# A new timetable for rounding the weights, its last product on another engine, and fewer feed-forward pieces a turn

## Chip, cores and metric

The kernel runs on one core of a Trainium2 chip. The metric is the device time of one execution in microseconds (us). Every quoted time of an instruction comes from one profiled execution of the kernel before the change, or is worked out from it. The engines are called PE (matrix products), DVE (vector), ACT (scalar activations), POOL (GpSimd) and SP (the queue that issues most transfers).

## What is computed

```python
# attention: q, k, v of shape (4, 8, 768, 64), centroids (8, 16, 64)
q_assign = argmax(q_n @ c_n, -1);  k_assign = argmax(k_n @ c_n, -1)
mask   = q_assign[:, :, :, None] == k_assign[:, :, None, :]
scores = where(mask, q @ k.T / sqrt(64), -1e9)
attn   = softmax(scores)
x      = (attn @ v) brought to (3072, 512)      # 4 batches of 768 rows
# feed-forward layer: w_in (512, 2048), w_out (2048, 512)
h   = x @ w_in
out = h * sigmoid(1.702 * h) @ w_out
```

The inputs `q`, `k`, `v` and the centroids are 32-bit. The two weight matrices come as 64-bit floating-point numbers: the kernel reads each as two 32-bit halves and has to turn them into 32-bit numbers itself before a matrix product can use them. The code calls this rounding.

## The kernel before

**Attention runs in turns.** There are 16 pairs of heads (four batches of four pairs), and each pair has two halves of its 768 query columns, which gives 32 groups. A group has six key tiles. One turn handles two key tiles, so a group takes three turns and the loop over `t` runs 98 times, of which 96 start new tiles. The first 24 turns (`TB`) belong to batch 0. In a turn the kernel issues, in this order: the score products (L393), for batch 0 an additional product that carries the cluster mask (L407), the exponentials on ACT (L418), the mask on DVE for the later batches (L429) and the sum over key tiles on POOL (L439), pieces of the preparation of later pairs (transposes L271 with their ACT copies L276, `prep_near` L285 to L291, `prep_assign` L302 to L325), and the value products of the turn before (L450). Every third turn `normalise` closes a group: PE adds over partitions (L462), DVE takes the reciprocal (L465) and multiplies (L467). `check` then reads that reciprocal on ACT (L477, L479). In batch 0 it is called in the same turn as `normalise`, later one turn after it.

**The feed-forward work is filled in between.** When group 3 has been normalised (turn 13), 28 pieces of work for the first half of batch 0 go into the queue `half_ffn`: 16 calls of `first` (product L516, tanh on ACT L486, the factor on DVE L487) and 12 of `second3` (product L496). After group 7 (turn 25) 48 pieces for the second half go into `ffn`. A running account, `owed`, decides how many pieces a turn takes: it grows by `rate` a turn while `half_ffn` lasts and by 0.62 a turn for `ffn`, of which the last eight pieces are left until attention has ended. Batches 1 to 3 are computed after attention, by functions that the change does not touch.

**Rounding a weight piece.** The weights are cut into 32 pieces of 128 x 512, 16 of `w_in` and then 16 of `w_out`. One call of `round_next` is a round. Round i issues the load of piece i+2 on SP (L155), splits piece i, and joins piece i-1. The split is two DVE operations (L168 takes the exponent bits, L170 the leading mantissa bits) and two ACT operations (L172, L174). The join is three DVE operations: L180 adds the sign, L183 adds the low half, L186 multiplies the two parts. There are 33 rounds. The buffers are three for `raw` (a loaded piece) and two for `e` (its exponent). `first` and `second3` call `round_to`, which makes up rounds that are still missing for the columns or rows that they read.

**When rounds are issued.** Before turn 12 there is one round in turns 1, 2, 4, 5, 6, 8, 9 and 10, at the end of the turn. From turn 12 on there are two a turn (one right after the exponentials, one before the feed-forward pieces) and a third one in odd turns, after them. The 33 rounds end in turn 21. The engines take their instructions strictly in this written order, each engine by itself, and wait for each other by semaphores:

```python
        for u in us:
            exps(u)
        second_half = t >= TB // 2
        if second_half:
            round_next()
        if recs:
            check(*recs)
```

Of the kernel before, what the change touches and what calls it, by code (L numbers as in the profile page):

```python
# [8 lines left out]
FP32 = mybir.dt.float32  # L9
# [5 lines left out]
ALU = mybir.AluOpType  # L15
# [3 lines left out]
def kernel(  # L19
    tc: tile.TileContext,  # L20
    q: bass.AP,
    k: bass.AP,
    v: bass.AP,
    centroids: bass.AP,
    moe_w_in: bass.AP,
    moe_w_out: bass.AP,
    out: bass.AP,
):

    args = (q, k, v, centroids, moe_w_in, moe_w_out, out)
    bad = fast(tc, *args)
    with tc.If(bad > 0):
        general(tc, *args)
# [3 lines left out]
def fast(  # L39
# [26 lines left out]
    nc = tc.nc  # L66
# [7 lines left out]
    NH = NJ // 2  # L74
# [3 lines left out]
    NF = DF // P  # L78
# [73 lines left out]
    def load_w(i):  # L152
        if i < NW:
            t = wp.tile([P, WN, 2], I32, name="raw")
            nc.sync.dma_start(out=t.rearrange("p n t -> p (n t)"),  # L155
                              in_=w_chunks[i][1])
            w_raw[i] = t
# [5 lines left out]
    def split_w(i):  # L163

        hi = w_raw[i][:, :, 1]
        w = w_chunks[i][0]
        e = wp.tile([P, WN], I32, name="e", bufs=2)
        nc.vector.tensor_scalar(out=e, in0=hi, scalar1=EXP, scalar2=None,  # L168
                                op0=ALU.bitwise_and)
        nc.vector.tensor_scalar(out=w.bitcast(I32), in0=hi, scalar1=0xFFFFF,  # L170
                                scalar2=None, op0=ALU.bitwise_and)
        nc.scalar.activation(out=e, in_=e, func=AF.Relu, scale=8.0,  # L172
                             bias=low[:, 0:1])
        nc.scalar.activation(out=w, in_=w.bitcast(I32), func=AF.Copy,  # L174
                             scale=2.0 ** -20, bias=1.0)
        w_pow[i] = e

    def join_w(i):
        raw, e, w = w_raw.pop(i), w_pow.pop(i), w_chunks[i][0]
        nc.vector.scalar_tensor_tensor(  # L180
            out=e, in0=raw[:, :, 1], scalar=-2 ** 31, in1=e,
            op0=ALU.bitwise_and, op1=ALU.bitwise_or)
        nc.vector.scalar_tensor_tensor(  # L183
            out=w, in0=raw.bitcast(U32)[:, :, 0], scalar=2.0 ** -52, in1=w,
            op0=ALU.mult, op1=ALU.add)
        nc.vector.tensor_tensor(out=w, in0=w, in1=e.bitcast(FP32),  # L186
                                op=ALU.mult)

    w_done = [0]

    def round_next():
        i = w_done[0]
        if i < NW:
            load_w(i + 2)
            split_w(i)
        if 0 < i <= NW:
            join_w(i - 1)
        w_done[0] += 1

    def round_to(n):  # L200
        while w_done[0] <= min(n, NW):
            round_next()
# [50 lines left out]
    for a in range(2):  # L253
        rows = slice(a * D, (a + 1) * D)
        nc.vector.tensor_copy(
            out=cT[rows, :, a, :],
# [130 lines left out]
    def scores(u):  # L387
        g, kt = divmod(u, NJ)
        p, h = split(g)
        ps = ps_s.tile([P, 2, 512], FP32, name="s")  # L390
        for a in range(2):
            rows = slice(a * D, (a + 1) * D)
            nc.tensor.matmul(out=ps[:, a, 0:HALF],  # L393
                             lhsT=T[p, 1][rows, kt * P:(kt + 1) * P],
                             rhs=T[p, 0][rows, h * HALF:(h + 1) * HALF],
                             start=True, stop=(p >= HP))
        s_of[u] = ps[:, :, 0:HALF]

    def part(u):

        g, kt = divmod(u, NJ)
        p, h = split(g)
        if p >= HP:
            return
        for a in range(2):
            r = 32 * (2 * (p % 2) + a)
            nc.tensor.matmul(  # L407
                out=s_of[u][:, a, :],
                lhsT=hots[p // 2, 1][r:r + NC, kt * P:(kt + 1) * P],
                rhs=hots[p // 2, 0][r:r + NC, h * HALF:(h + 1) * HALF],  # L410
                start=False, stop=True)

    def exps(u):
        p, h = split(u // NJ)
        s = s_of[u]
        if p < HP:
            A_of[u] = ap.tile([P, 2, HALF], FP32, name="A")
        nc.scalar.activation(out=A_of[u] if p < HP else s, in_=s, func=AF.Exp,  # L418
                             scale=SCALE)

    def mask(u):

        g, kt = divmod(u, NJ)
        p, h = split(g)
        s = s_of.pop(u)
        if p >= HP:
            A_of[u] = ap.tile([P, 2, HALF], FP32, name="A")
            for a in range(2):
                nc.vector.scalar_tensor_tensor(  # L429
                    out=A_of[u][:, a, :],  # L430
                    in0=qcode[p][:, a, h * HALF:(h + 1) * HALF],
                    scalar=code[p][:, kt % NH, 1, kt // NH, a:a + 1],
                    in1=s[:, a, :], op0=ALU.is_equal, op1=ALU.mult)
        A = A_of[u]
        if kt == 0:
            return
        if kt == 1:
            sum_of[g] = ap.tile([P, 2, HALF], FP32, name="sum", bufs=2)
        nc.gpsimd.tensor_tensor(out=sum_of[g],  # L439
                                in0=A_of[u - 1] if kt == 1 else sum_of[g],  # L440
                                in1=A, op=ALU.add)

    def values(u):
        g, kt = divmod(u, NJ)
        p, h = split(g)
        if kt == 0:
            o_of[g] = ps_o.tile([P, 512], FP32, name="o")
        A = A_of.pop(u)
        for a in range(2):
            nc.tensor.matmul(out=o_of[g][a * D:(a + 1) * D, 0:HALF],  # L450
                             lhsT=v_in[p][:, a, kt, :], rhs=A[:, a, :],
                             start=(kt == 0), stop=(kt == NJ - 1))
        if kt == NJ - 1:
            O_of[g] = xp.tile([P, HALF], FP32, name="x")
            nc.scalar.copy(O_of[g], o_of.pop(g)[:, 0:HALF])
# [15 lines left out]
    recs = {}  # L471

    def check(g):


        rec = recs.pop(g)
        nc.scalar.activation(out=rec, in_=rec, func=AF.Copy,  # L477
                             accum_out=row_sums[:, 0, g:g + 1])
        nc.scalar.activation(out=rec, in_=rec, func=AF.Relu, bias=top[:, 0:1],  # L479
                             scale=-2.0 * LIMIT * LIMIT,  # L480
                             accum_out=row_sums[:, 1, g:g + 1])
# [22 lines left out]
    half_ffn, ffn = deque(), deque()  # L504
# [63 lines left out]
    NT = NU // 2  # L568
    TG = NJ // 2
    TB = 2 * HP * TG  # L570

    prep_at = {}
    for p in range(1, NPAIR):
        b, hp = divmod(p, HP)
        for i in range(2 if p == 1 else 0, len(PREP)):
            if p == 1:
                t = (i - 2) // 2
            elif b == 0:
                t = (hp - 2) * TG + 1 + i // 2
            else:  # L580
                t = b * TB + TG * hp - (7, 7, 6, 6, 4, 3, 2)[i]
# [5 lines left out]
    def prep(p, i):  # L587
        if i == 0 and p:
            load_v(p)
        PREP[i](p)  # L590
        if i in (1, 3) and loads:
            load_qk(*loads.popleft())

    rate = (NF + NH * (NF // 4)) / (TB / 2 - 0.5)
    owed = 0.0
    for p, i in [(0, i) for i in range(6)] + [(1, i) for i in range(2)]:
        prep(p, i)
# [2 lines left out]
    for t in range(NT + 2):  # L600
        us = range(2 * t, 2 * t + 2) if t < NT else ()
        for u in us:
            scores(u)
        if t == 0:
            prep(0, 6)
        for u in us:
            part(u)
        for u in us:
            exps(u)
        second_half = t >= TB // 2  # L610
        if second_half:
            round_next()
        if recs:
            check(*recs)
        for u in us:
            mask(u)
        work = sorted(prep_at.get(t, ()), key=lambda w: PREP[w[1]] != prep_near)
        while work and PREP[work[0][1]] == prep_near:
            prep(*work.pop(0))
        if 1 <= t <= NT:  # L620
            for u in range(2 * t - 2, 2 * t):
                values(u)

        todo = half_ffn or (ffn if len(ffn) > NF // 2 else ())
        owed += (rate if half_ffn else 0.62) if todo else -owed
        g = (t - 2) // TG if t >= 2 and (t - 2) % TG == TG - 1 else None
        if g is not None and second_half:
            normalise(g)
        for p, i in work:
            prep(p, i)  # L630
        if g is not None and not second_half:
            normalise(g)
        if recs and t < TB:
            check(*recs)
        if second_half or t and t % 4 != 3:
            round_next()
        while owed >= 1 and todo:
            todo.popleft()()
            owed -= 1
        if second_half and t % 2:  # L640
            round_next()
    check(*recs)
    qcode.clear()
    att.close()
# [181 lines left out]
    for b in range(1, B):  # L826
# [5 lines left out]
        for n in range(NH):  # L832
            sg = sums_g(n)
            if (b, n) == (B - 1, 1):
# [3 lines left out]
                                        op=ALU.min)  # L838
# [454 lines left out]
```

## Time and profile before

| what | value |
|---|---|
| median of three runs | 1054.43 us (1050.65 to 1055.23) |
| run that was profiled | 1050.77 us, span of its instructions 1048.9 us |
| PE busy | 996.9 us (95%) |
| DVE busy | 686.5 us (65%) |
| POOL busy | 389.3 us (37%) |
| ACT busy | 365.3 us (35%) |
| first turn starts / turn 14 / turn 27 / last turn | 11.4 / 87.7 / 253.5 / 582.8 us |

The first three rows are the clock of the whole kernel; the busy times are those of single engines in the profiled execution, and they overlap. The last row is read from the score products (L393) in the timeline, eight of whose records belong to a turn. A PE that is busy is not idle, but it can run at a reduced clock, so the granted clock has to be read beside it.

### The profile page before, as it was taken

The numbers are of one execution on the slowest core, as the hardware profiler recorded it, in microseconds if no ns is written. First come the engines' busy times: TensorE is split into PE (matmuls) and PEld (weight loads), VectorE is DVE, ScalarE is ACT, GpSimd is POOL, SyncE is SP. The second block draws the span as 40 slices with busy tenths as digits, with TensorE's granted clock in tenths as the row PEclk, the third lists the DMA queues.
The fourth block names the chain that finished last, engine by engine and source line by source line (L and its number), as shares of the span: only waits on it lengthen the run. The fifth ranks groups of instructions, "written<-read, shape, count | busy, mean of one in ns | idle before, by whom it ended". The sixth has DMA issues, their size and how long they took to land.

```text
span 1048.9 us, 12464 instructions
## 1 busy us (share of the span) xinstructions
PE 996.9 (95%) x4574; PEld 583.3 (56%) x4574; DVE 686.5 (65%) x1079; ACT 365.3 (35%) x697; POOL 389.3 (37%) x280
## 2 busy tenths in 40 slices
PE   7878798999999999999999899999999999999997
PEld 4323353445544455444554355688755788655886
DVE  3899998415876788776877667743477634576431
ACT  4655465324555455455555322200022200122000
POOL 2655222223666456655567847600022100120000
PEclk9998899999999999999999999999999999999999
DMA  8423354112002320022000000000000000000000
GB/s 219 130 64 117 120 158 139 35 53 63 17 0 63 82 71 8 25 70 59 26 1 1 1 11 0 1 21 21 21 0 1 1 21 21 21 0 1 21 21 23
DMA packets 66117, 45.24 MB, mean 43 GB/s; under 512 B 52096, under 2 KB 60032, under 8 KB 66048
## 3 DMA queue, kind: packets, MB, share of 16 engines
q1 hardware_dynamic: 65904, 44.33, 14.9%
q8 instruction: 38, 0.62, 0.3%
q14 instruction: 31, 0.25, 0.1%
q10 hardware_dynamic: 144, 0.03, 0.0%
HBM read 38.04 MB, written 6.31 MB: 42 GB/s over the span
## 4 chain that ended last, share of the span: by engine, by line
PE 82%; DVE 12%; ACT 3%; issue 1%; DMA 1%; POOL 1%; SPq 0%; DVEq 0%; ACTq 0%; POOLq 0%
PE b L790 21%; PE b L733 21%; PE s L393 11%; PE o L450 9%; PE m L496 8%; PE m L545 4%; DVE short L465 3%; PE m L516 2%; DVE A L429 2%; PE m L271 2%; PE m L462 2%; DVE e L168 1%; PE m L285 1%; DVE e L180 1%; DVE w_in L186 1%
## 5 line engine op out<-in xcount | busy, mean ns | idle before, releaser
L439 POOL TENSOR_TENSOR sum<-sum,A 128x768 f32<-128x768 f32 x128 | 235.8, 1842 | 199.8 <-DVE A L429 104.5
L429 DVE SCALAR_TENSOR_TENSOR A<-qb,code,s 128x384 f32<-128x384 uint8 x288 | 157.7, 608 | 94.7 <-ACT s L418 79.6
L393 PE MATMUL s<-T,T 64*128 64x384 f32 x768 | 157.1, 521 | 13.2 <-ACT A L418 9.0
L450 PE MATMUL o<-A,inv 128*64 128x384 f32 x768 | 147.1, 502 | 1.1 <-DVE A L429 1.1
L418 ACT ACTIVATE s<-s 128x768 f32<-128x768 f32 x144 | 109.4, 793 | 83.4 <-PE s L393 72.6
L724 DVE TENSOR_TENSOR G<-b,G 128x384 f32<-128x384 f32 x168 | 93.4, 556 | 51.8 <-PE b L733 45.0
L671 POOL TENSOR_TENSOR W<-w_in 128x256 f32<-128x256 f32 x24 | 17.7, 738 | 263.7 <-PE b L733 262.8
L393 PEld LDWEIGHTS s<-T,T 64*128 64x128 f32 x768 | 65.6, 188 | 86.2 <-issue 23.0
L724 DVE TENSOR_TENSOR y<-b,y 128x256 f32<-128x256 f32 x54 | 22.1, 423 | 130.0 <-PE b L790 93.8
L486 ACT ACTIVATE th<-G 128x384 f32<-128x384 f32 x96 | 50.2, 523 | 158.9 <-DVE G L724 98.4
L733 PE MATMUL b<-x,w_in 128*128 128x384 f32 x288 | 101.2, 486 | 0.0
L450 PEld LDWEIGHTS o<-A,inv 128*64 128x64 f32 x768 | 47.1, 137 | 86.7 <-issue 81.5
L439 POOL TENSOR_TENSOR sum<-A 128x768 f32<-128x768 f32 x32 | 59.6, 1863 | 92.6 <-ACT A L418 43.1
L465 DVE RECIPROCAL short<-m 128x384 f32<-128x384 f32 x32 | 81.7, 2553 | 13.7 <-PE m L462 13.6
L487 DVE SCALAR_TENSOR_TENSOR G<-th,G 128x384 f32<-128x384 f32 x96 | 68.6, 714 | 16.8 <-ACT th L486 14.2
L733 PEld LDWEIGHTS b<-x,w_in 128*128 128x128 f32 x288 | 54.7, 190 | 37.9 <-issue 0.5
L733 PE MATMUL b<-x,W 128*128 128x384 f32 x192 | 69.8, 486 | 0.0
L516 PE MATMUL m<-x,w_in 128*128 128x384 f32 x128 | 51.4, 560 | 15.5 <-ACT short L291 4.9
L790 PE MATMUL b<-Z,G 128*128 128x256 f32 x288 | 65.1, 379 | 0.0
L790 PE MATMUL b<-w_out,G 128*128 128x256 f32 x288 | 63.6, 379 | 0.0
L790 PEld LDWEIGHTS b<-w_out,G 128*128 128x128 f32 x288 | 54.6, 190 | 8.1
L496 PE MATMUL m<-w_out,g 128*128 128x512 f32 x120 | 58.7, 613 | 0.2 <-ACT T L276 0.2
(115 smaller groups left out, 1306.0 us busy)
## 6 DMA issues: line engine op xcount, KB each, us to landing
raw<-in_moe_w_in_dram SPq DMA_DIRECT2D x16, 512.0 KB, 3.6
raw<-in_moe_w_out_dram SPq DMA_DIRECT2D x16, 512.0 KB, 3.6
in<-in_q_dram SPq DMA_DIRECT2D x32, 192.0 KB, 3.0
in<-in_k_dram SPq DMA_DIRECT2D x32, 192.0 KB, 4.0
inv<-in_v_dram SPq DMA_DIRECT2D x16, 384.0 KB, 3.9
out_dram<-y SPq DMA_DIRECT2D x15, 256.0 KB, 2.1
qb<-line SPq DMA_DIRECT2D x12, 192.0 KB, 3.1
out_dram<-y SPq DMA_DIRECT2D x18, 128.0 KB, 1.8
```

Source lines behind the costliest of these rows:

```text
L393: nc.tensor.matmul(out=ps[:, a, 0:HALF], lhsT=T[p, 1][rows, kt * P:(kt + 1) * P], rhs=T[p, 0][rows, h * HALF:(h + 1) * HALF], start=True, ...
L418: nc.scalar.activation(out=A_of[u] if p < HP else s, in_=s, func=AF.Exp, scale=SCALE)
L429: nc.vector.scalar_tensor_tensor(out=A_of[u][:, a, :], in0=qcode[p][:, a, h * HALF:(h + 1) * HALF], scalar=code[p][:, kt % NH, 1, kt // NH ...
L439: nc.gpsimd.tensor_tensor(out=sum_of[g], in0=A_of[u - 1] if kt == 1 else sum_of[g], in1=A, op=ALU.add)
L450: nc.tensor.matmul(out=o_of[g][a * D:(a + 1) * D, 0:HALF], lhsT=v_in[p][:, a, kt, :], rhs=A[:, a, :], start=(kt == 0), stop=(kt == NJ - 1))
L465: nc.vector.reciprocal(out=rec, in_=ps[:, 0:HALF])
L487: nc.vector.scalar_tensor_tensor(out=g, in0=t, scalar=1.0, in1=h, op0=ALU.add, op1=ALU.mult)
L496: nc.tensor.matmul(out=ps[:, 0:DM], lhsT=g, rhs=w_out[:, f, :], start=(f == 0), stop=(f == NF - 1))
L516: nc.tensor.matmul(out=ps[:, 0:HALF], lhsT=w_in[:, c, f * P:(f + 1) * P], rhs=xT[c], start=(c == 0), stop=(c == NCH - 1))
L724: nc.vector.tensor_tensor(out=o, in0=p, in1=a, op=ALU.add)
L733: nc.tensor.matmul(out=ps[:, 0:HALF], lhsT=a[:, c], rhs=x(c), start=(c == 0), stop=(c == 1))
L790: nc.tensor.matmul(out=ps[:, 0:DN], lhsT=a(f // 4)[:, f % 4], rhs=z(f), start=(f == 0), stop=(f == FB - 1))
```

## The change

`join_w` is told which engine multiplies (L186): DVE up to turn 13, POOL from turn 14 on. The rounds follow a table, `pace`: one round in turns 0, 2, 5, 8, 9, 11, 12 and 13, then two rounds in every turn from turn 14 until all are done. A round of the first group stands right after the exponentials of its turn instead of at the end (turn 13: at the end); of the later pairs, one stands after the exponentials and one after the feed-forward pieces. The 33rd round falls in turn 26. The second call of `check` in batch 0's turns goes, so that `check` always runs one turn after `normalise`. `half_ffn` is taken at 1.6 pieces a turn instead of 28/11.5 = 2.43, which ends it in turn 31 instead of turn 25, and `ffn` at 0.65 instead of 0.62. The number of instructions of each kind is the same.

```diff
-    def join_w(i):
+    def join_w(i, engine):
         raw, e, w = w_raw.pop(i), w_pow.pop(i), w_chunks[i][0]
...
-        nc.vector.tensor_tensor(out=w, in0=w, in1=e.bitcast(FP32),
-                                op=ALU.mult)
+        engine.tensor_tensor(out=w, in0=w, in1=e.bitcast(FP32), op=ALU.mult)
...
-    def round_next():
+    def round_next(engine=nc.gpsimd):
...
-            join_w(i - 1)
+            join_w(i - 1, engine)
...
-    rate = (NF + NH * (NF // 4)) / (TB / 2 - 0.5)
+    rate = 1.6
+
+
+    pace = {t: 1 for t in (0, 2, 5, 8, 9, 11, 12, 13)}
+    pace.update((t, 2) for t in range(TB // 2 + 2, NT))
...
         second_half = t >= TB // 2
-        if second_half:
-            round_next()
+        dense = t >= TB // 2 + 2
+        if pace.get(t) and t != TB // 2 + 1:
+            round_next(nc.gpsimd if dense else nc.vector)
...
-        owed += (rate if half_ffn else 0.62) if todo else -owed
+        owed += (rate if half_ffn else 0.65) if todo else -owed
...
-        if recs and t < TB:
-            check(*recs)
-        if second_half or t and t % 4 != 3:
-            round_next()
         while owed >= 1 and todo:
             todo.popleft()()
             owed -= 1
-        if second_half and t % 2:
-            round_next()
+        if pace.get(t) == 2 or t == TB // 2 + 1:
+            round_next(nc.gpsimd if dense else nc.vector)
```

## The prediction, made before the changed kernel was run

> **What bounds the kernel now.** I read the slices of the span first, then busy times by stage cut at turn starts (turn 0 at 11.4 us, 14 at 87.7, 20 at 165.5, 27 at 253.5), then the waits, and last the timelines of PE, DVE and POOL where PE stands still. The slices:
>
> ```profile
> PE   7878798999999999999999899999999999999997
> DVE  3899998415876788776877667743477634576431
> POOL 2655222223666456655567847600022100120000
> PEclk9998899999999999999999999999999999999999
> ```
>
> A slice is 26 us. PE has room only in the first seven or so, up to about 190 us, and there DVE is full. The stages (columns: stretch, length, then PE, PEld, DVE, ACT, POOL, clock, DMA):
>
> ```profile
> 42.00:87.70 45.70, 36.65 (x205) 13.82 (x203) 42.44 (x50) 29.17 (x53) 26.51 (x13) 0.89 0.30 90
> 87.70:165.50 77.80, 67.17 (x252) 32.70 (x252) 74.40 (x103) 40.27 (x76) 23.22 (x12) 0.91 0.43 131
> 165.50:253.50 88.00, 81.84 (x329) 37.09 (x328) 39.05 (x60) 30.18 (x58) 21.22 (x12) 0.98 0.25 70
> 253.50:560.00 306.50, 300.15 (x1718) 146.91 (x1718) 236.06 (x362) 160.12 (x303) 185.62 (x104) 1.00 0.15 39
> ```
>
> From 42 to 253.5 us PE idles 9.1 + 10.6 + 6.2 = 25.8 us, and the clock withheld is worth 0.11 x 45.7 + 0.09 x 77.8 + 0.02 x 88 = 13.8 us more. After that PE sets the pace, so at most 39.6 us can be won, 3.8%. What PE waits for in this part, and what ACT waits for (turns 5 to 21):
>
> ```profile
> ACT e L172 <- DVE e L168: 24.1, 15, 3.1
> ACT short L477 <- DVE x L467: 21.9, 6, 4.4
> ...
> PE s L393 <- ACT A L418: 9.0, 4, 3.2
> ```
>
> DVE holds ACT, in rounding and in `check`, and ACT's exponentials then hold PE. Why DVE is full shows in its timeline beside POOL's (start, length):
>
> ```profile
> 63.20 3.85 POOL L439 TENSOR_TENSOR sum<-sum,A 128x768 f32<-128x768 f32 x2 [2.78 <-ACT A L418]
> 63.47 1.92 DVE L168 TENSOR_SCALAR e<-raw 128x512 int32<-128x512 int32 x1
> 65.31 2.03 DVE L170 TENSOR_SCALAR w_in<-raw 128x512 int32<-128x512 int32 x1
> 67.27 0.67 DVE L180 SCALAR_TENSOR_TENSOR e<-raw,e 128x512 int32<-128x512 int32 x1
> ```
>
> L168 and L170 take 0.42 us by their medians; here each lasts until one of POOL's two sums ends. DVE's rounding and POOL exclude each other.
>
> **What the Trainium skill says.** "SBUF — State Buffer", section Who interferes with whom: a GpSimd operation and a DVE one with two SBUF inputs, or in a two-port mode, take turns, each for its whole length; DVE operations with one SBUF input and no such mode are free. The trace agrees: 1.92 against 0.42 us, while the reciprocal (2.55 us) and the mask (0.609 us) keep their length beside POOL. "GPSIMD Engine Reference", section 3.1, gives some 2.5 cycles an element for two inputs; here 768 elements take 1.812 us and 256 take 0.727, 2.1 ns an element. "Perfetto Trace Analysis", section Optimizing Scalar/DVE Operations, warns that moving work between these two engines might not help. "TensorE: Matmul & The Clock Gate", Part 1, halves PE's clock after an idle window of about 3.4 us; here a turn's score products take 2.93 us after a 3.0 us gap at 63.1 us, against 1.56.
>
> **The change part by part.**
>
> *Prices.* A round on DVE takes 2.72 us from start to start (41.86 to 44.58 us): split 0.68, L180 and L183 1.31, L186 0.73. The product on POOL is in no trace: between the two widths above, 512 elements give 0.727 + 256 x 2.12 ns = 1.27 us; the rows of POOL that read `w_out` take 1.048 for 256, which would give 1.59. Nothing excludes a shorter time, but no row is faster per element. I take 1.27. A gelu factor (L487) is 0.56 us, a `normalise` 3.2, an assignment 2.2, a mask 0.61 on DVE; a sum 1.81 on POOL.
>
> *How far POOL and DVE overlap.* From 87.7 to 165.5 us: 17 rounds 46.2, 12 factors 6.7, three normalisations 9.6, 12 sums 21.7: 84.2 us in 77.8. So 6.4 of POOL's 21.7 us (30%) lay beside DVE work.
>
> *Turns 0 to 13.* Before, 13 rounds are issued, now 8: five less, 13.6 us of DVE. But turns 5, 8 and 11, each after a `normalise`, now have the round right behind the exponentials, so that ACT's L172 waits for DVE as `check` did. Turn 5: reciprocal from 38.1 us, its product to about 41.3, then L168 and L170 each behind a sum, to 45 or 46; ACT then does L174, `check` (1.5 us) and the copies to 48.5, which `prep_near` on PE needs; before, that product started at 48.39. Turns 8 and 11 by the same steps let turn 10 start at 66.7 (before 67.9), turn 13 at about 81.3 (83.5) and turn 14 at 85.7 (87.7). So moving `check` behind the exponentials gives almost nothing, and the stage gains 2 us; nothing is lost unless round 0 is too early for its data. Its load is issued at 7.8 us and L168 could start at 14.7 us; landing takes 3.6 us on a quiet queue. Bounds: 0 to 2 us; I take 0, since turn 1's late rounds had nothing to wait for either. On SP the load of piece 2 moves ahead of one load of a pair that is transposed only in turn 4. The larger gain is in what DVE owes: x of group 3 is ready at 89 us, against 96.8 before, and no `first` has to wait for it.
>
> *Turns 14 to 26, the block that decides.* DVE, from the end of `normalise`(3): 24 splits and 25 joins without product 16.3 + 32.8, round 7 still on DVE 2.7, 16 factors 9.0, four normalisations 12.8, two assignments 4.4, 12 masks 7.3: 85.3 us. POOL: 22 sums 39.8 and 25 products 31.8: 71.6. In series that is 157 us; with 30% of POOL beside other work, 135. The least is 157 minus the DVE work that POOL does not hinder (factors, reciprocals, masks, most of the assignments: 30 us), 127. PE in the same turns: ten times 3.57 and three times 3.07 for attention, 16 `first` at 2.67, four `second3` at 3.45, normalising 3.2, transposes and assignment of pairs 4 to 7 15.9: 120.4 us, less than DVE with POOL.
>
> *A wait is added.* With two buffers for `e`, L168 of round i needs POOL's product of piece i-2, which is issued in the round just before. The second round of a turn is followed on DVE by the first of the next, so L168 waits at least 1.3 us, and behind it every later DVE operation and ACT's L172. It is the time for which the shared port would have held L168 anyway, so I count it once. POOL's sums queue behind the products; they are wanted two turns later, so that costs nothing. Pieces of `w_in` are ready turns ahead of their `first`; the last `second3` of the first tile, in turn 26, reads piece 31 of the same turn: 0 to 2 us, 0.5 taken.
>
> *Sum.* 135 us from 89 end at 224 for DVE; PE's turn 27 needs no rounding any more and can start some 7 us earlier, at 216.5. Eight `second3` (27.6 us) and one piece of `ffn` (2.0) are still to be done there that were done before: 246.1 against 253.5, 7.4 us less. From turn 27 to 31 PE has 10 us of work a turn, DVE half, so nothing is lost; the pace 0.65 lets `ffn` reach turn 92 instead of 88 and may save 1 us of the bare turns at the end. In all about 8 us: 1041 against the span of 1048.9. The profiled run (1050.8) lies at the low end of the three; against their median, 1054.4 - 8.4 = 1046.
>
> **The rivals.** *PE keeps the pace.* If POOL's products fall beside reciprocals, masks and DVE's waits for PE, the block takes PE's 120.4 from 85.7: turn 27 at 206, 235.7 against 253.5, 18 less: 1036; with the stalls of turns 6 to 12 gone as well, 1027. For it: DVE is then often waiting, and POOL is free in that time. Against: PE has only 1.1 us to spare a turn.
>
> *DVE and POOL in series: slower.* L168 behind the product of the round before, and that product behind the sums in POOL's order, leave no overlap. Then the block takes 157, turn 27 starts at 238, and 267.7 against 253.5 is 14 more: 1068; with products of 1.59 us, 1076. It decides from where less than 20% of POOL's time is beside other work (143 us for the block). For it: the added wait ties every second product to DVE. Against: the 30% measured before.
>
> *It evens out.* 20 to 28% overlap, or half-clock stretches at small gaps in turns 14 to 19: 1050 to 1059. That the change fails to do what it says I exclude: it moves named instructions.
>
> **How the numbers follow.** The main case (1040 to 1052) gets 0.48, PE's pace 0.22, evening out 0.12, series 0.18. Of the main case 0.10 lies within 0.5% (5.3 us, about what a measurement of this kernel can tell from no change), 0.38 below. Faster: 0.38 + 0.22 = 0.60; the same: 0.10 + 0.11 = 0.21; slower: 0.01 + 0.18 = 0.19. The range reaches into both outer cases, to 1028 and 1064, and leaves out the lowest of the one and the upper half of the other, about 0.14. Main case alone: 1040 to 1052.
>
> **What would show it.** Right: turn 14 starts at 84 to 87, turn 27 at 212 to 221, turn 32 near 263; products on POOL of 1.2 to 1.6 us; L168 idle or stretched by about 1.3 us once a turn; `first` no longer waiting for L467. Wrong: turn 27 after 224 (series), or before 209 with PE without gaps (PE's pace); or a gain in turns 0 to 13 above 5 us, which would mean that `check` had mattered.

## The result and the profile after

The changed kernel takes 1065.74 us (median of four runs, 1065.08 to 1068.97), the one before 1054.79 us. The ratio is 1.0119, with a 95% interval of 1.0086 to 1.0152: it is slower by some 12.5 us. The execution that was profiled is the slowest of the four (1068.97 us, span 1067.2), and the profiled one of before lay near its fastest, so the two traces are 18.3 us apart. What follows accounts for these 18.3; what an edit wins or loses is taken from the ratios.

The slices of the changed kernel, in the order of those shown above:

```profile
PE   7788796889999999999999899999999999999997
DVE  3567855584467687777777757743477725476432
POOL 2444554443356556665566757700022100121000
PEclk9889987899999999999999999999999999999999
```

In the first nine slices, up to 240 us, DVE is nowhere full now (3 to 8), and PE in one of them alone. The stages, cut at this kernel's own turns (turn 14 starts at 97.0 us, 27 at 245.3, 32 at 292.5; columns as before):

```profile
42.00:97.00 55.00, 45.81 (x253) 17.63 (x249) 38.95 (x39) 29.01 (x52) 30.24 (x17) 0.88 0.23 63
...
97.00:245.30 148.30, 124.05 (x500) 57.25 (x498) 94.79 (x151) 71.21 (x135) 74.45 (x48) 0.90 0.38 114
...
245.30:292.50 47.20, 46.96 (x175) 19.76 (x174) 22.93 (x34) 12.58 (x23) 14.54 (x9) 1.00 0.08 25
```

The middle row is the block of turns 14 to 26. PE is idle for 24.3 of its 148.3 us, and a clock of 0.90 takes up to another 14.8 us (an estimate, 0.10 of 148.3); DVE works for 94.8 and POOL for 74.5 us. No single engine is the bound. Against before:

| start of | before | after | difference |
|---|---|---|---|
| turn 2 | 21.9 | 22.9 | +1.0 |
| turn 4 | 32.7 | 39.7 | +6.9 |
| turn 14 | 87.7 | 97.0 | +9.3 |
| turn 27 | 253.5 | 245.3 | -8.1 |
| turn 32 | 278.2 | 292.5 | +14.4 |
| last turn | 582.8 | 601.3 | +18.5 |

Of the first line 0.4 us lie before turn 0. Part of the fourth is spread between executions: turn 14 starts between 93.3 and 98.0 us in the other kernels below whose turns 0 to 13 are those of the changed kernel, and in `slow_pace`, which has those of before, at 89.9. The block is 17.5 us shorter than before, but it leaves eight `second3` and one piece of `ffn` to later turns, whose stage grows by 22.5 us (47.2 against 24.7). The tail, from turn 32 on, gives a little back.

Two stalls of PE show the two causes. The first is in turn 2. The timeline of PE, then that of DVE:

```profile
26.96 0.55 PE L270 MATMUL m<-ident,in 128*128 128x128 f32 x3
31.99 0.90 PE L270 MATMUL m<-ident,in 128*128 128x128 f32 x3 [4.48 <-DVE qb L362]
```

```profile
25.41 0.42 DVE L168 TENSOR_SCALAR e<-raw 128x512 int32<-128x512 int32 x1
25.76 0.42 DVE L170 TENSOR_SCALAR w_in<-raw 128x512 int32<-128x512 int32 x1
26.09 2.31 DVE L180 SCALAR_TENSOR_TENSOR e<-raw,e 128x512 int32<-128x512 int32 x1
28.33 2.29 DVE L183 SCALAR_TENSOR_TENSOR w_in<-raw,w_in 128x512 f32<-128x512 uint32 x1
30.65 0.69 DVE L186 TENSOR_TENSOR w_in<-w_in,e 128x512 f32<-128x512 f32 x1
31.37 0.56 DVE L362 COPY qb<-m 64x768 bf16<-64x768 bf16 x1
```

(Lines of the changed kernel are one lower from L186 on, up to the feed-forward part.) PE's transposes wait for a PSUM bank (PE writes its results into PSUM, and a bank must be copied out before it is written again) that the copy L362 of `prep_hot` must empty. Round 1 now stands in front of that copy, and two of its operations are held by POOL's sums (2.31 and 2.29 us instead of 0.68).

The second is in turn 20. ACT's timeline, then PE's line at its end:

```profile
161.87 0.72 ACT L172 ACTIVATE e<-e,low 128x512 int32<-128x512 int32 x1 [4.58 <-DVE e L168]
162.50 0.61 ACT L174 ACTIVATE w_out<-w_out 128x512 f32<-128x512 int32 x1
163.02 1.49 ACT L417 ACTIVATE A<-s 128x768 f32<-128x768 f32 x2
165.21 0.72 ACT L172 ACTIVATE e<-e,low 128x512 int32<-128x512 int32 x1 [0.70 <-DVE e L168]
165.84 0.61 ACT L174 ACTIVATE w_out<-w_out 128x512 f32<-128x512 int32 x1
...
167.61 0.46 ACT L290 COPY short<-m 128x384 f32<-128x384 f32 x1
```

```profile
168.12 1.65 PE L515 MATMUL m<-x,w_in 128*128 128x384 f32 x2 [6.41 <-ACT short L290]
```

ACT does its part of the second round of turn 19, the exponentials, its part of the first round of turn 20, then `check`, and only then the copies L290 and L275 that give PE its banks back. Each part of a round waits for DVE's split, and that one for POOL (DVE's waits in the block):

```profile
DVE x L486 <- ACT x L485: 30.2, 9, 7.5
DVE e L168 <- POOL w_out L186: 9.7, 7, 1.4
DVE e L168 <- POOL w_in L186: 5.5, 4, 1.4
```

PE, ACT, DVE and POOL hand the turn round in a ring, and each stands still for part of it. Of the 24.3 us that PE is idle in the block, 20.3 are waits of the feed-forward products (L515, L495) for L290 or L275.

### The profile page after: what moved, and what is told of

Its sections match the earlier page's. It is cut to its first block, busy times and chain, and to the rows that moved or that the text cites. A ratio compares the mean times of both kernels' runs of the same rounds, so it can differ in the third digit from the quotient of the medians.

```text
span 1067.2 us, 12458 instructions
## 1 busy us (share of the span) xinstructions
PE 1007.6 (94%) x4574; PEld 586.1 (55%) x4574; DVE 659.8 (62%) x1054; ACT 364.8 (34%) x697; POOL 418.6 (39%) x305
## 4 chain that ended last, share of the span: by engine, by line
PE 84%; DVE 9%; ACT 3%; issue 2%; POOL 2%; DMA 0%; DVEq 0%; ACTq 0%; POOLq 0%
PE b L790 20%; PE b L733 20%; PE s L392 11%; PE o L449 10%; PE m L495 8%; PE m L544 4%; PE m L515 3%; PE m L270 2%; DVE e L168 2%; PE m L461 2%; DVE short L464 2%; PE m L284 1%; DVE e L180 1%; POOL w_out L186 1%; PE m L295 1%
## 5 line engine op out<-in xcount | busy, mean ns | idle before, releaser
L671 POOL TENSOR_TENSOR W<-w_in 128x256 f32<-128x256 f32 x24 | 17.7, 739 | 263.7 <-PE b L733 263.2
L464 DVE RECIPROCAL short<-m 128x384 f32<-128x384 f32 x32 | 81.7, 2552 | 12.2 <-PE m L461 12.1
L486 DVE SCALAR_TENSOR_TENSOR G<-th,G 128x384 f32<-128x384 f32 x96 | 68.4, 713 | 17.1 <-ACT th L485 14.4
L515 PE MATMUL m<-x,w_in 128*128 128x384 f32 x128 | 54.2, 581 | 18.5 <-ACT short L290 10.1
L790 PE MATMUL b<-w_out,G 128*128 128x256 f32 x288 | 63.6, 379 | 0.0
L495 PE MATMUL m<-w_out,g 128*128 128x512 f32 x120 | 60.0, 625 | 3.3 <-ACT T L275 3.3
```

The source lines that it names most:

```text
L464: nc.vector.reciprocal(out=rec, in_=ps[:, 0:HALF])
L486: nc.vector.scalar_tensor_tensor(out=g, in0=t, scalar=1.0, in1=h, op0=ALU.add, op1=ALU.mult)
L495: nc.tensor.matmul(out=ps[:, 0:DM], lhsT=g, rhs=w_out[:, f, :], start=(f == 0), stop=(f == NF - 1))
L515: nc.tensor.matmul(out=ps[:, 0:HALF], lhsT=w_in[:, c, f * P:(f + 1) * P], rhs=xT[c], start=(c == 0), stop=(c == NCH - 1))
L790: nc.tensor.matmul(out=ps[:, 0:DN], lhsT=a(f // 4)[:, f % 4], rhs=z(f), start=(f == 0), stop=(f == FB - 1))
```

## The experiments

Each kernel's ratio is to the kernel before, run on the same chip in between, with its 95% interval. The changed kernel stands at 1.0119.

**The early rounds.** In `early_end` the rounds of turns 0 to 12 go back to the end of their turns; in `late2` only that of turn 2.

```diff
-        if pace.get(t) and t != TB // 2 + 1:
-            round_next(nc.gpsimd if dense else nc.vector)
+        if dense and pace.get(t):
+            round_next(nc.gpsimd)
...
-        if pace.get(t) == 2 or t == TB // 2 + 1:
+        if pace.get(t) and (not dense or pace[t] == 2):
             round_next(nc.gpsimd if dense else nc.vector)
```

> The changed kernel with the rounds of turns 0 to 12 at the end of their turns, where the kernel before had its early rounds; the calendar and all else stay. Theory 1 (the round of turn 2 stands in front of pair 1's hot copy on DVE, and PE waits 4.5 us for a bank): turn 3 starts at 27 to 28 us instead of 32.8, and 5 to 7 us are kept to the end: about 1059. Theory 2 (what counts is the dense part alone, and time lost early is taken back there because DVE catches up): turn 14 starts earlier, but the end moves by less than 2 us: 1064 to 1066.

1.0017 (1.0007 to 1.0027), 1054.8 us: theory 1, and some 4 us more than it asked for. Turn 3 starts at 26.8 us and turn 14 at 82.0 instead of 97.0, and the block then takes 147.8 us as in the changed kernel. The copy stands in front of the round again:

```profile
25.66 0.56 DVE L362 COPY qb<-m 64x768 bf16<-64x768 bf16 x1 [0.82 <-PE m L357]
26.25 0.59 DVE L168 TENSOR_SCALAR e<-raw 128x512 int32<-128x512 int32 x1
```

> The changed kernel with the round of turn 2 alone at the end of its turn; the rounds of turns 0, 5, 8, 9, 11 and 12 stay right behind the exponentials. Theory 1 (in the early stage turn 2 is the loss: its round delays a PSUM bank that PE waits for): turn 3 starts at 26 to 28 us, and 5 to 7 of the 11 us come back, 1059 to 1061. Theory 2 (rounds right behind the exponentials hold ACT in turns 5, 8 and 11, and turn 2 only shifts that): 1064 to 1066 although turn 3 starts earlier.

1.0058 (1.0039 to 1.0077), 1060.1 us: about half of it. Turn 14 starts at 90.0 us. That is theory 1: turn 2 costs about 6 us. The other half of what `early_end` won, about 5 us, lies in the rounds right behind the exponentials of the other early turns. Three stalls of PE in turns 6, 9 and 12, of 2.6, 3.5 and 2.9 us in the changed kernel, are the same in `late2` within 0.1 us and shrink to 1.4, 2.3 and 2.3 us in `early_end`; the second is, in the changed kernel:

```profile
74.35 2.35 PE L392 MATMUL s<-T,T 64*128 64x384 f32 x8 [3.53 <-ACT A L417]
```

**Who multiplies.** `dve_mult` puts all products on DVE, `mult2_dve` only that of a turn's second round.

```diff
 # dve_mult
-        engine.tensor_tensor(out=w, in0=w, in1=e.bitcast(FP32), op=ALU.mult)
+        nc.vector.tensor_tensor(out=w, in0=w, in1=e.bitcast(FP32), op=ALU.mult)
 # mult2_dve
         if pace.get(t) == 2 or t == TB // 2 + 1:
-            round_next(nc.gpsimd if dense else nc.vector)
+            round_next(nc.vector)
```

> The changed kernel with the last product of every piece on DVE again (0.7 us there instead of 1.27 us on POOL); calendar and pace stay. Theory 1 (PE, ACT and DVE run in turn, because ACT's copies stand behind both rounds' ACT part; the product on POOL lengthens the loop once a turn by about 1.4 - 0.7 us): 13 turns by 0.7 make 5 to 9 us less, 1057 to 1061. Theory 2 (POOL relieves a DVE that is full, so giving the product back costs 25 by 0.7 us): up to 10 us more, 1070 to 1076.

> The changed kernel with the product of every second round of a turn on DVE, so that the exponent of the next round no longer waits for a POOL product issued just before; the product of the first round stays on POOL. If the added wait is what costs: 13 turns by 0.7 us or more, 1053 to 1057. If the loop through ACT stays as long as it is without that wait, or the waiting is passed on to the shared port: 1063 to 1066.

`dve_mult`: 1.0198 (1.0176 to 1.022), 1073.5 us, so theory 1 as stated falls; the number is that of theory 2, but not, as `order_only` below shows, for its reason. `mult2_dve`: 1.0003 (0.9989 to 1.0018), 1053.5 us: the added wait does cost what was supposed. L168's waits for POOL, 15.2 us, are gone, and the block takes 136.8 us instead of 148.3. The product of the second round on POOL is a loss of some 12 us, that of the first round a gain of some 20. A saving of 13 times 0.7 us of DVE doesn't explain 20, so I formed another theory: the first round's product stands in POOL's order in front of the turn's sums. It waits for DVE's join, and so the sums start only when DVE has done with its round and no longer hold its operations. Without it, in `dve_mult`, a sum starts beside the round (a line of POOL, then two of DVE):

```profile
129.61 3.76 POOL L438 TENSOR_TENSOR sum<-sum,A 128x768 f32<-128x768 f32 x2 [8.19 <-ACT A L417]
...
129.80 1.92 DVE L168 TENSOR_SCALAR e<-raw 128x512 int32<-128x512 int32 x1
131.64 2.02 DVE L170 TENSOR_SCALAR w_in<-raw 128x512 int32<-128x512 int32 x1
```

`order_only` tests that. It is `mult2_dve` with 496 of 512 columns of the first round's product on DVE as well; POOL multiplies the last 16.

```diff
-        engine.tensor_tensor(out=w, in0=w, in1=e.bitcast(FP32), op=ALU.mult)
+        f, k = e.bitcast(FP32), WN if engine is nc.vector else WN - 16
+        nc.vector.tensor_tensor(out=w[:, 0:k], in0=w[:, 0:k], in1=f[:, 0:k],
+                                op=ALU.mult)
+        if k < WN:
+            engine.tensor_tensor(out=w[:, k:], in0=w[:, k:], in1=f[:, k:],
+                                 op=ALU.mult)
```

> The changed kernel with the second round's product on DVE, and of the first round's product 496 of 512 columns on DVE too; only the last 16 columns are left to POOL. Theory 1 (the first round's product on POOL helps because it stands in front of the sums in POOL's order, so that the sums start after DVE's join and do not hold its operations; where the work is done matters little): near the run with whole products there, 1053 to 1059, against 1073.5 with all products on DVE. Theory 2 (it helps because it takes 0.7 us of work a turn from DVE): near the run with all products on DVE, 1069 to 1074.

1.0009 (0.9994 to 1.0024), 1054.4 us: with hardly any of the multiplying left on POOL the gain is whole. The groups of DVE in the block, first of `dve_mult`, then of `order_only` (count, then busy us and mean ns):

```profile
L180 DVE SCALAR_TENSOR_TENSOR e<-raw,e 128x512 int32<-128x512 int32 x26 | 22.6, 870 | 0.0
L168 DVE TENSOR_SCALAR e<-raw 128x512 int32<-128x512 int32 x25 | 21.0, 841 | 0.4
L170 DVE TENSOR_SCALAR w_out<-raw 128x512 int32<-128x512 int32 x16 | 13.1, 820 | 0.0
L170 DVE TENSOR_SCALAR w_in<-raw 128x512 int32<-128x512 int32 x9 | 8.6, 958 | 0.0
```

```profile
L180 DVE SCALAR_TENSOR_TENSOR e<-raw,e 128x512 int32<-128x512 int32 x26 | 17.8, 683 | 0.0
L168 DVE TENSOR_SCALAR e<-raw 128x512 int32<-128x512 int32 x25 | 12.0, 481 | 0.4
L170 DVE TENSOR_SCALAR w_out<-raw 128x512 int32<-128x512 int32 x16 | 6.7, 418 | 0.0
L170 DVE TENSOR_SCALAR w_in<-raw 128x512 int32<-128x512 int32 x9 | 5.4, 598 | 0.0
```

The same instructions, 65.3 us against 41.9. The sums now meet other operations of DVE, such as L471 (1.24 us by its mean, against 0.59 for the same one, L466, in `dve_mult`), but those are few. The timeline of `order_only`, one line of DVE and then POOL's:

```profile
151.05 0.68 DVE L187 TENSOR_TENSOR w_out<-w_out,e 128x496 f32<-128x496 f32 x1
...
151.09 0.71 POOL L190 TENSOR_TENSOR w_out<-w_out,e 128x16 f32<-128x16 f32 x1 [6.85 <-DVE w_out L183]
151.76 3.69 POOL L443 TENSOR_TENSOR sum<-sum,A 128x768 f32<-128x768 f32 x2
```

The prediction quoted a warning that moving work between these two engines might not help. Here the same work helped in one place of the turn and harmed in the other.

**The place of the dense round.** A dense turn is one with two rounds, 14 or later. `prep_first` issues the first round of turns 14 and later behind the preparation steps, so that ACT's copies and `check` go first.

```diff
-        if pace.get(t) and t != TB // 2 + 1:
-            round_next(nc.gpsimd if dense else nc.vector)
+        if pace.get(t) and t < TB // 2 + 1:
+            round_next(nc.vector)
...
             prep(p, i)
+        if dense and pace.get(t):
+            round_next(nc.gpsimd)
```

> The changed kernel with the first round of a dense turn (14 on) issued behind the preparation steps and before the feed-forward pieces, so that ACT copies the transposes and runs check before its part of that round; the product stays on POOL. Theory 1 (PE waits for banks whose ACT copies stand behind the round): the waits of the feed-forward product for those copies, some 20 us in turns 17 to 25, go to under 6, the block of turns 14 to 26 falls from 148 to 130 to 138 us, 1050 to 1056. Theory 2 (the exponent's wait for POOL's product sets the block wherever the round stands): tanh and factor then stand behind the round instead, the block stays at 144 to 150, 1062 to 1067.

1.0056 (1.0038 to 1.0074), 1058.5 us, and a block of 138.3 us: nearer to theory 1, without reaching its time. PE's waits for L290 and L275 fall from 20.3 to 11.9 us in the feed-forward products, but 4.1 us appear before the transposes, and the sums reach DVE's rounding again: L168, L170, L180 and L183 together take 78.2 us in the block instead of 64.0.

**The pace of the pieces.** `fast_rate` takes the changed kernel back to 28/11.5 and 0.62; `slow_pace` gives the kernel before 1.6 and 0.65.

```diff
-    rate = 1.6
+    rate = (NF + NH * (NF // 4)) / (TB / 2 - 0.5)
...
-        owed += (rate if half_ffn else 0.65) if todo else -owed
+        owed += (rate if half_ffn else 0.62) if todo else -owed
```

> The changed kernel with 28/11.5 pieces a turn for the first half-block and 0.62 for the second, as before the change. Theory 1 (a turn with two rounds takes 10 to 11 us whatever PE has to do, so fewer pieces a turn leave PE idle): PE is filled in turns 14 to 25, its idle time between 98 and 245 us falls from about 25 us to under 10, and the end comes 8 to 16 us earlier, 1050 to 1058. Theory 2 (the port shared by POOL and DVE sets the block, and the gelu factors only add to it): the turns become longer by as much as PE gains, 1063 to 1068.

1.0194 (1.0174 to 1.0215), 1073.2 us: worse than either theory said, for a reason in neither. The pieces overtake the calendar of rounds (`pace`), `round_to` makes the missing rounds up in front of `second3`, and PE waits for each product on POOL:

```profile
PE m L495 <- POOL w_out L186: 14.9, 7, 5.6
```

PE is idle for 22.9 us between 98 and 245 us, not for under 10. So this run doesn't decide between the theories; it shows that the pace is tied to the calendar.

> The kernel before with the new pace of the feed-forward pieces alone (1.6 and 0.65), its own rounds and products. Theory 1 (fewer pieces a turn leave PE with nothing to do while a DVE-bound turn lasts): the turns of the rounds get hardly shorter, because rounds and not factors fill DVE; 6 to 12 us more, 1060 to 1066. Theory 2 (spreading the half-block into turns in which PE has room is a gain by itself): 1 to 5 us less than before, 1048 to 1053.

1.0073 (1.0056 to 1.0091), 1060.2 us: theory 1 by its number, though the turns did get shorter. With the rounds of before, the slower pace alone is a loss of 7 to 8 us: turn 27 comes 17.7 us earlier, but with some 29 us more of PE work still to do.

**`check`.** `check_late` takes only the second call of `check` from the kernel before.

```diff
-        if recs and t < TB:
-            check(*recs)
```

> The kernel before without its second call of check in batch 0's turns, so that check follows one turn after the normalisation; nothing else. The prediction's step (nothing to win, since the round behind the exponentials holds ACT in the same way) was argued with the new places of the rounds; with the old places, at the end of the turn, theory 1: the exponentials of the next turn no longer stand behind the reciprocal, the three stalls of 2.4 to 3.2 us before turns 6, 9 and 12 shrink, and 3 to 8 us are won, 1045 to 1050. Theory 2: DVE's backlog passes the wait to ACT's part of the rounds: within 2 us of before.

1.0023 (1.0014 to 1.0031), 1055.7 us: theory 2, with a small loss of some 2 us. The stalls move from before turns 6, 9 and 12 to before turns 6, 10 and 12 (1.5, 2.7 and 2.3 us), and another of 2.7 us stands before turn 14.

**Together.** `combo` has the edits of `early_end` and `mult2_dve`, `combo_prep` that of `prep_first` as well, and `before_order` brings the finding on POOL's order into the kernel before, in the first round of turns 12 and later, all else as it was.

```diff
 # before_order; in join_w the product is split as in order_only
         if second_half:
-            round_next()
+            round_next(WN - 16)
```

> The changed kernel with both edits of the runs before: rounds of turns 0 to 12 at the end of their turns, and the product of a turn's second round on DVE. If early and dense stage lose independently (11 and 12 us by those runs), their gains add: 1042 to 1046. If they share a cause, such as time lost early being waited out later, the gain is that of one alone: 1052 to 1055.

> The best kernel so far (early rounds at the end of the turn, second round's product on DVE, 1043) with the first round of a dense turn behind the preparation steps. If the waits of the feed-forward product for ACT's copies in turns 17 to 25 (12 us still) come from the round standing in front of those copies: 4 to 9 us less, 1034 to 1039. If the place of POOL's product in front of the sums mattered more, which this edit gives up: 1043 to 1050.

> The kernel before, with the last 16 of 512 columns of the product left to POOL in the first round of every turn from 12 on; rounds, pace and check as before. Theory 1 (a product in front of the sums in POOL's order keeps the sums off DVE's rounding, whatever else the change does): DVE's round operations between 88 and 254 us lose most of the 18 us by which sums lengthen them, and 6 to 14 us are won, 1040 to 1048. Theory 2 (this works only with rounds spread as in the changed kernel; here a third round in odd turns and DVE's backlog let the sums collide with another round): within 3 us of before.

`combo`: 0.9903 (0.9884 to 0.9922), 1043.0 us: the two losses are independent and their gains add. `combo_prep`: 0.9906 (0.9887 to 0.9925), 1042.6 us: nothing on top. Its block takes 136.4 us, `combo`'s 137.6 and `prep_first`'s 138.3, so two edits that each shorten the block don't add. They may shorten the same ring; but `combo_prep` also gives up the place in front of the sums, and L168, L170, L180 and L183 take 74.8 us in its block against 63.6 in `combo`. No run keeps the two apart. `before_order`: 0.9921 (0.9906 to 0.9936), 1045.0 us: sixteen columns on POOL are worth 8 us without anything else of the change. The sums' hold on DVE shrinks less than theory 1 asked for, though: the round operations between 87.7 and 253.5 us take 80.2 us, with two more of them in that stretch, instead of 84.8.

## Why the prediction was wrong

*What bounds the kernel* fits the runs: relieving DVE of POOL's sums alone won 8 us (`before_order`). *The price of the product on POOL* was right (1.27 us against medians of 1.270 for `w_in` and 1.272 for `w_out` in the trace).

*Turns 0 to 13* failed. The prediction had turn 14 at 85.7 us, 2 less than before; it came at 97.0. Its step "nothing is lost unless round 0 is too early for its data" looked at the wrong round and the wrong resource. Round 0 did little harm (turns 0 and 1 take 11.1 us instead of 10.5); round 1, moved in turn 2 ahead of `prep_hot`, kept PE waiting 4.5 us for a bank. That instruction stood in the same turn of the code, and I had not listed what queues behind the moved round on DVE there. For turns 5, 8 and 11 I had found that ACT's part of the round takes over `check`'s wait, and counted that as even with before. That much held for `check` (`check_late`), but not for the rounds: the ends of the turns were worth some 5 us more (`late2` against `early_end`). So x of group 3 was ready at 100.3 us, not at 89.

*The block* failed in its method. I added DVE's and POOL's work, let 30% overlap as measured before, and took the 135 us for the time, since PE had less. From 85.7 us that put turn 27 at 216.5, 130.8 us for the block; it took 148.3. The 30% came from a stage in which DVE was full. Here DVE waited 30.2 us for tanh and 15.2 for POOL's products, and the sum of one pair of engines no longer says how long the turn is: the order in which four engines wait for each other came in, and the prediction's sum had no term for it.

*The added wait*: "the time for which the shared port would have held L168 anyway, so I count it once". `mult2_dve` shows otherwise: without that wait, by giving half of POOL's products back to DVE, the block is 11.5 us shorter.

*The rival in series* gave 1068 us, near what was measured, and its test (turn 27 after 224) was met. That is luck in part. It had named the right wait, L168 behind the product of the round before, but not the rest: it let DVE and POOL fill 157 us between them, whereas both stood still for much of the block, and it had nothing for turn 2: its block was 9 us too long and the turns before it 11 us too short.

*Turn 27 and the rest*: turn 27 came 8.1 us earlier than before, and the 29.6 us of work left over are then 21.5 us too many. The slower pace pays only if the block shrinks by as much as it leaves over; with the old rounds it lost 7 to 8 us by itself (`slow_pace`). *The tail* gave some 4 us where 1 was taken: from turn 32 to the last turn the lag grows by only 4.1 us, although four pieces of `ffn`, 8 us, that were behind are made up. PE is idle there for some 3 us less than before, about half of it in the last three turns.

Of the 18.3 us between the traces, turns 0 to 13 are 9.3, the block with the work it leaves (29.6 - 17.5) 12.1, and the tail about -3. What remains open is why the block stays at 136 to 138 us in `mult2_dve`, `order_only`, `combo` and `combo_prep`, with PE idle for some 17 us of it.

## What to carry to other kernels

Before moving a step, list for every engine the instructions between its old and its new place, and ask of each what it frees: one 0.56 us copy that empties a bank was worth 6 us here. Where engines work in order and wait for each other in a ring, adding up two of them gives no time; follow one turn round all of them. Where two engines exclude each other, as DVE's rounding and POOL's sums do here, it helped to keep one from starting in the middle of the other's work, and a tiny instruction that waits for the right moment, put in front of its long ones, can do that.

## What was not expected of the hardware

The 16-column product on POOL takes 0.71 us, against 1.27 us for 512 columns, but that is not its own price. Each of the 13 in `order_only` starts within 0.05 us of DVE's product of the other 496 columns (0.67 us) and ends 0.08 us after it, so it seems to spend most of its time waiting for DVE. What such a product costs alone, no run shows.

When PE stands still, its clock is halved for a while. In the changed kernel's trace gaps up to 1.4 us brought none of this, and gaps of 2.4 us and more did, shorter ones than the idle window of about 3.4 us that the prediction quoted. The halved stretches last 3.4, 6.8 or 10.2 us, but the gap alone doesn't say which. The stall of 4.5 us in turn 2 is followed by 6.8 us at half clock in the changed kernel and by 3.4 us in `order_only`. Before the change a gap of 3.0 us at 108 us brought 6.8 us, and one of 4.9 us at 171 us brought 3.4. Half of such a stretch is lost where PE has work: by this estimate the 3.5 us stall at 70.8 us, with 6.8 us behind it, cost up to 6.9 us, about twice its length.
